# More fillers at the start, an earlier last attention product, and a smaller feed-forward share in one stage of a fused attention and feed-forward kernel

## The chip, the cores and the metric

The kernel runs on one core of a Trainium2 chip. The metric is the device time of one execution in microseconds (us). Times are medians of several runs. A ratio is the mean time of one kernel's fast runs over the mean time of the other's fast runs of the same rounds, so it is not quite the ratio of the medians that are quoted beside it.

## The reference

Grouped-query attention, then a feed-forward layer with squared ReLU, over 8 batches. There are 16 query heads and 4 key/value heads of dimension 64, and 384 positions in each batch.

```python
scores = (q @ k.T) / sqrt(64)              # k and v repeated for groups of 4 heads
attn   = softmax(scores)
x      = (attn @ v)                        # laid out as 3072 tokens x 1024
h      = maximum(x @ w_in, 0)              # w_in: 1024 x 2048
out    = (h * h) @ w_out                   # w_out: 2048 x 1024
```

The inputs and the output are 32-bit floats; the loads on the GpSimd queue convert them to bf16 on their way (the load of one batch's k, 98304 numbers, moves 192.0 KB into `k_st`), apart from the first batch's q, k and v, which are converted by engines.

## The kernel before

A helper records every operation with what it reads and writes. It puts each engine's operations in program order and adds the semaphore waits. So **each engine works strictly in the order of the program text**. Two heads make a "pair": 8 pairs per batch, numbered `n` from 0 over all batches. "b0" is batch 0 (pairs 0 to 7), "b1" batch 1 (pairs 8 to 15), "b2" batch 2.

The feed-forward of one batch lags one batch behind its attention. It is a generator of small steps: up tiles (`x @ w_in`, 8 matmuls each) and down tiles (`h² @ w_out`, 16 matmuls each). `fill(ns)` takes steps from it until their estimated time is used up. Its results alternate between two banks of PSUM (the memory that matmuls write), `f_ps0` and `f_ps1`. `xT` is the transposed attention output that the up tiles read.

```python
    PER_PAIR = {1: 3700.0, **{b: 5100.0 for b in range(2, B + 1)}}
    ...
    # b0: no feed-forward exists yet; idle(n) issues n matmuls on a zeroed tile ("fillers")
    def idle(count):
        def mm(pe):
            for _ in range(count):
                m = pe.matmul(f_ps[1][:, 0:256], warm[:, 0:128], warm[:, 0:256])
            return m
        R.add("tensor", mm, reads=["warm"], writes=[("f_ps", 1)])
    ...
    # from b1 on
    for n in range(NPB, NP + 1):                 # NPB = 8 pairs per batch
        per = PER_PAIR[n // NPB]
        if n < NP:
            scores_pair(n)                       # q k^T, then one exponential on ScalarE
        fill(per * 0.4)
        if n > NPB:
            attend(n - 1, 0)                     # attention x v on TensorE (AV)
        fill(per * 0.2)
        if n > NPB:
            attend(n - 1, 1)                     # AV, then 1/sum and product on VectorE
            landed = put_x(n - 1)                # transpose by DMA into xT, on the sync queue
            ...
        if n % NPB == 4 and n // NPB + 1 < B:
            prepare(n // NPB + 1)                # k duplicate on VectorE, then DMA transposes
        if n % NPB == 7 and n // NPB + 1 < B:
            prepare_v(n // NPB + 1)
        fill(per * 0.4)
        ready[0] = max(0, n // NPB - 1)          # whose feed-forward may start
```

A down tile ends with a copy of its bank to SBUF (the working memory on the chip) on VectorE ("y copy") and a store. The big loads all wait in one queue, in this order:

```python
    ... # w_in in 8 parts, v of b1 among them
    for i in range(2):
        load_w_out(i)
    load_k(2)
    load_q(2)
    load_v(2)
```

The softmax here doesn't subtract the row's maximum and nothing guards it: scores larger than these inputs give would overflow.

Of the kernel before, what the change touches and what calls it, by code (L numbers as in the profile page):

```python
# [106 lines left out]
def bass_gqa_attention__then__ffn_squared_relu_kernel(  # L107
# [11 lines left out]
    B, H, S, D = 8, 16, 384, 64  # L119
# [4 lines left out]
    NPB = H // 2  # L124
# [145 lines left out]
# [7 lines that stand above are left out]
# [11 lines left out]
    RING, FREE = (4, 5, 6), (0, 1, 2, 3)  # L288
# [9 lines left out]
    def turn_on_pe(src, src_keys, dst, dst_keys, banks, eng="vector", n=NJ):  # L298
        ps, key = turn_bank(banks)

        def tr(pe):
            for t in range(n):
                m = pe.matmul(ps[:, t * 128:(t + 1) * 128], src[:, t * 128:(t + 1) * 128], ident[:],  # L303
                              is_transpose=True)
            return m

        R.add("tensor", tr, reads=[*src_keys, "ident"], writes=[key])
        if eng == "scalar":
            R.add(eng, lambda e: e.copy(dst, ps[:, 0:n * 128]), reads=[key], writes=dst_keys)
        else:  # L310
            R.add(eng, lambda e: e.tensor_copy(dst, ps[:, 0:n * 128]), reads=[key], writes=dst_keys)  # L311

    def first_kT(g, b=0, banks=RING, j0=0, j1=NJ):
        turn_on_pe(k_dup[b][:, g * NJ + j0:g * NJ + j1].rearrange("p a x d -> p (a x d)"),
                   [("k_dup", b, g, j) for j in range(j0, j1)], kT[b][:, g, j0 * 128:j1 * 128],
                   [("kT", b, g, j) for j in range(j0, j1)], banks, n=j1 - j0)

    def first_qT(c, b=0, banks=RING):
        turn_on_pe(q_st[b][:, 2 * c:2 * c + 2, :].rearrange("p h e -> p (h e)"), [("q_st", b, c)],
                   qT[b][:, c], [("qT", b, c)], banks)  # L320

    def first_oT(c, banks=RING, eng="vector"):
        turn_on_pe(o_sb[c % NO].ap().rearrange("p i s d -> p (i s d)"), [("o_sb", c % NO, x) for x in range(2)],
                   xT[0][:, c], [("xT", 0, c)], banks, eng)

    def dup_all_k(b, eng="vector"):
        src = k_st[b % NKS].ap().rearrange("p g j d -> p (g j) d").unsqueeze(2)
        R.add(eng, lambda e: e.tensor_copy(  # L328
            k_dup[b % 2][:, :, :, :], src.to_broadcast([128, HKV * NJ, 2, D])),
            reads=[("k_st", b % NKS)], writes=[("k_dup", b % 2, g, j) for g in range(HKV) for j in range(NJ)])  # L330
# [26 lines left out]
    def scores_unit(p, j):  # L357
        u = (p * NJ + j) % 2
        kt, qt, keys, k_keys = operands(p)
        keys = keys + k_keys[j:j + 1]  # L360

        def sc(pe):
            for x in range(2):
                rows = slice(64 * x, 64 * x + 64)
                m = pe.matmul(sc_ps[:, 2 * u + x, 0:S], kt[rows, j * 128:(j + 1) * 128], qt[rows, :])  # L365
            return m

        R.add("tensor", sc, reads=keys, writes=[("sc", 2 * u), ("sc", 2 * u + 1)])
        src = sc_ps[:, 2 * u:2 * u + 2, 0:S].rearrange("p x (t c) -> p x t c", t=NJ)
        dst = expT[p % NEX][:, j, :].rearrange("p (t x c) -> p x t c", x=2, t=NJ)  # L370
        R.add("scalar", lambda e: e.activation(dst, src, AF.Exp, scale=0.125),  # L371
              reads=[("sc", 2 * u), ("sc", 2 * u + 1)], writes=[("expT", p % NEX, j)])
# [29 lines left out]
    def attend(p, s, alone=False):  # L402
        b, g = p // NPB, (p % NPB) // 2
        acc, acc_key = (po_alt, ("sc", 1)) if alone and s == 1 else (po_v, "po")

        def av(pe):
            for i in range(NJ):
                f = NJ * s + i
                for j in range(NJ):
                    m = pe.matmul(acc[:, i, s, :], expT[p % NEX][:, j, f * 128:(f + 1) * 128],  # L410
                                  v_aug[b % 2][:, g * NJ + j, :], start=(j == 0), stop=(j == NJ - 1))
            return m

        R.add("tensor", av, reads=[("expT", p % NEX, j) for j in range(NJ)] +
              [("v_aug", b % 2), ("v_one", b % 2)], writes=[acc_key])
        if alone or s == 1:
            ss = slice(s, s + 1) if alone else slice(0, 2)
            w = ss.stop - ss.start
            rinv_v = rinv[p % 2][:, :, ss].unsqueeze(3)
            R.add("vector", lambda e: e.reciprocal(rinv_v, acc[:, :, ss, D:D + 1]),  # L420
                  reads=[acc_key], writes=[("rinv", p % 2)])
            rb = rinv_v.to_broadcast([128, NJ, w, D])
            R.add("vector", lambda e: e.tensor_tensor(o_sb[p % NO][:, :, ss, :], acc[:, :, ss, 0:D], rb, ALU.mult),  # L423
                  reads=[acc_key, ("rinv", p % 2)], writes=[("o_sb", p % NO, s)])
# [70 lines left out]
    def all_feed_forward():  # L495
        for b in range(B):
            while ready[0] < b:
                yield None
            yield from feed_forward(b)

    ffn = all_feed_forward()
    credit = [0.0]
    PER_PAIR = {1: 3700.0, **{b: 5100.0 for b in range(2, B + 1)}}

    def fill(ns):
        credit[0] += ns
# [7 lines left out]
    turns = [lambda banks=RING, g=g: first_kT(g, 1, banks) for g in range(HKV)]  # L514
    turns += [lambda banks=RING, c=c: first_qT(c, 1, banks) for c in range(NPB)]

    idle(13)
    first_kT(0, banks=(4,), j1=1)
    idle(1)
    first_qT(0, banks=(6,))  # L520
    for n in range(NPB):
        ring = (4, 6) if n < 4 else RING
        scores_unit(n, 0)
        if n >= 4:
            turns.pop(0)()
        elif n == 0:
            first_kT(0, banks=(4,), j0=1)
            idle(2)
        else:
            idle(1)  # L530
        if n >= 1:
            attend(n - 1, 0)
        scores_unit(n, 1)
        if n % 2 == 1 and n + 1 < NPB:
            first_kT((n + 1) // 2, banks=ring)
        if n + 1 < NPB:
            first_qT(n + 1, banks=ring)
        if n == 3:
            dup_all_k(1)
        if n >= 1:  # L540
            attend(n - 1, 1)
        scores_unit(n, 2)
        if n < 4:
            idle(1)
        if n >= 2:
            first_oT(n - 2, ring)
        if n in (4, 6, 7):
            turns.pop(0)()
    for _ in range(3):
        next(ffn)  # L550
    attend(NPB - 1, 0, True)
    first_oT(NPB - 2, (4,), "scalar")
    attend(NPB - 1, 1, True)
    for _ in range(5):
        next(ffn)
    first_oT(NPB - 1, (0,))
    for _ in range(4):
        next(ffn)
    prepare_v(1)
    while turns:  # L560
# [2 lines left out]
    for n in range(NPB, NP + 1):  # L563
        per = PER_PAIR[n // NPB]
        if n < NP:
# [49 lines left out]
```

## Time and profile before

| | before |
|---|---|
| median of the first three runs | 440.08 us |
| span of the profiled run | 437.8 us |
| TensorE busy | 431.2 us |
| TensorE's waits that the profile names | 4.1 us |

PE is TensorE, PEld its weight loads, DVE VectorE, ACT ScalarE, POOL GpSimd, SPq the sync engine's DMA queue. The granted clock (PEclk) is the share of TensorE's full clock that the profile records as allowed. First the busy table and the chain of work that ended last, of the kernel before:

```profile
PE 431.2 (98%) x3631; PEld 240.7 (55%) x3631; DVE 164.3 (38%) x357; ACT 199.5 (46%) x210; POOL 34.4 (8%) x50
...
PE 97%; DVE 2%; DMA 1%; issue 0%
```

TensorE looks like the whole story. Its list of waits (waiting line, what released it, total us, times, longest us):

```profile
PE f_ps L441 <- DMA xT<-o_sb: 1.3, 1, 1.3
PE f_ps L273 <- DVE warm L221: 1.1, 1, 1.1
PE f_ps L441 <- DVE qT L311: 0.7, 1, 0.7
```

The first is the last transpose of b1's attention output, which the up tiles of b1 need. The third is a copy that must leave the bank of the first up tile. The change aims at both.

Less visible is the state of the other engines at 60 to 68 us. The timeline, before (start us, duration us, engine, line, operation, count, and in brackets idle time just before it and what ended it):

```profile
60.58 0.69 DVE L467 COPY y_sb<-f_ps 128x512 f32<-128x512 f32 x1 [3.84 <-PE f_ps L459]
...
61.41 0.56 DVE L423 TENSOR_TENSOR o_sb<-po,rinv 128x384 bf16<-128x384 f32 x1
...
65.38 1.89 PE L459 MATMUL f_ps<-w_out_sb,h2T 128*128 128x512 bf16 x8
...
65.94 0.56 DVE L328 COPY k_dup<-k_st 128x1536 bf16<-128x1536 bf16 x1 [3.98 <-DMA k_st<-in_k_dram]
66.42 0.68 DVE L467 COPY y_sb<-f_ps 128x512 f32<-128x512 f32 x1
...
67.20 0.66 PE L382 MATMUL sc_ps<-qT,kT 64*128 64x128 bf16 x9
...
67.80 1.90 PE L459 MATMUL f_ps<-w_out_sb,h2T 128*128 128x512 bf16 x8
```

VectorE stands for 3.98 us at the k duplicate, because b2's k comes late, behind all weights. This costs nothing here: the first y copy is ahead of the duplicate in program order, at 60.58 us, so its bank is free when the third down tile starts at 65.38 us. The scores at 67.20 us are those of pair 14, and the second half of that tile follows them at 67.80 us.

The loads go on up to 76 us: the DMA share is 1.23 to 1.57 in the stretches of 5 us from 41 to 76 us, and 0.99 from 76 to 81. The table by stretch, before (busy us and instructions of each engine, granted clock, DMA share, GB/s):

```profile
core 0: us, PE busy (x) PEld busy (x) DVE busy (x) ACT busy (x) POOL busy (x), PEclk, DMA share, GB/s
61.00:66.00 5.00, 5.00 (x46) 2.51 (x44) 0.99 (x4) 2.09 (x1) 0.00 (x0) 1.00 1.41 215
66.00:71.00 5.00, 5.00 (x46) 2.55 (x45) 2.99 (x7) 2.09 (x1) 0.00 (x0) 1.00 1.57 161
...
86.00:91.00 5.00, 5.00 (x46) 3.06 (x44) 2.33 (x5) 1.57 (x3) 0.00 (x0) 1.00 0.09 35
```

A share above 1 means that the times of the packets overlap: 1.57 while the loads run, 0.09 after them.

### The profile page before, as it was taken

How to read it: one execution, taken by the hardware profiler on the slowest of the kernel's cores; microseconds unless marked ns; L12 is line 12 of the kernel's file. 1: busy time of each engine (PE TensorE's matmuls, PEld its weight loads, DVE VectorE, ACT ScalarE, POOL GpSimd, SP SyncE). 2: the span in 40 equal slices, each digit the busy share in tenths (PEclk: the TensorE clock that was granted, in tenths of full speed). 3: DMA queues.
4: the chain of work that ended last, by engine and by line, in shares of the span. 5: the costliest groups of instructions: out<-in, count | busy, mean ns of one | idle time of the engine just before them, and what ended most of it. 6: DMA issues, size and time to landing. Idle time of an engine off the chain costs nothing.

```text
span 437.8 us, 8262 instructions
## 1 busy us (share of the span) xinstructions
PE 431.2 (98%) x3631; PEld 240.7 (55%) x3631; DVE 164.3 (38%) x357; ACT 199.5 (46%) x210; POOL 34.4 (8%) x50
## 2 busy tenths in 40 slices
PE   8999999899999999999999999999999999999997
PEld 4555654466545654466555565456654565545544
DVE  2555424244224442334432453234422444224412
ACT  4856753456433663256433555326642466203400
POOL 4940000020000200020000200002000000000000
PEclk9999999999999999999999999999999999999999
DMA  7999999757722937229622576229442100220012
GB/s 219 172 197 202 192 204 168 178 59 79 150 91 67 114 69 130 67 69 115 123 83 70 74 98 143 66 91 113 64 112 91 58 20 18 67 82 24 1 54 89
DMA packets 96083, 44.70 MB, mean 102 GB/s; under 512 B 74416, under 2 KB 90032, under 8 KB 96048
## 3 DMA queue, kind: packets, MB, share of 16 engines
q0 software_dynamic: 34288, 16.65, 30.5%
q1 hardware_dynamic: 58720, 25.28, 25.3%
q10 hardware_dynamic: 3040, 2.26, 1.7%
q8 instruction: 28, 0.46, 0.4%
q14 instruction: 7, 0.06, 0.0%
HBM read 35.65 MB, written 12.58 MB: 110 GB/s over the span
## 4 chain that ended last, share of the span: by engine, by line
PE 97%; DVE 2%; DMA 1%; issue 0%
PE f_ps L459 39%; PE f_ps L441 38%; PE po L410 8%; PE sc_ps L382 7%; PE sc_ps L365 1%; PE f_ps L273 1%; PE sc_ps L303 1%; PE f_ps L303 1%; DMA xT<-o_sb 1%; DVE o_sb L423 1%; DVE qT L311 0%; DVE xT L311 0%; PE sc_ps L441 0%; DVE kT L311 0%; DVE rinv L420 0%
## 5 line engine op out<-in xcount | busy, mean ns | idle before, releaser
L441 PE MATMUL f_ps<-xT,w_in_sb 128*128 128x384 bf16 x1016 | 181.4, 326 | 2.1 <-DMA xT<-o_sb 1.3
L459 PE MATMUL f_ps<-w_out_sb,h2T 128*128 128x512 bf16 (+2 forms) x784 | 180.3, 375 | 0.0
L399 ACT ACTIVATE expT<-sc_ps 128x2304 bf16<-128x2304 f32 x56 | 116.8, 2085 | 100.9 <-PE sc_ps L382 99.1
L441 PEld LDWEIGHTS f_ps<-xT,w_in_sb 128*128 128x128 bf16 x1016 | 92.4, 98 | 63.3 <-issue 6.4
L450 ACT ACTIVATE h2T<-hr 128x384 bf16<-128x384 f32 x128 | 66.6, 521 | 105.5 <-DVE hr L448 104.0
L459 PEld LDWEIGHTS f_ps<-w_out_sb,h2T 128*128 128x128 bf16 x784 | 70.2, 98 | 75.7 <-issue 5.5
L448 DVE TENSOR_SCALAR hr<-f_ps 128x384 f32<-128x384 f32 x127 | 70.5, 556 | 101.1 <-PE f_ps L441 101.1
L467 DVE COPY y_sb<-f_ps 128x512 f32<-128x512 f32 (+2 forms) x49 | 33.3, 680 | 104.9 <-PE f_ps L459 104.5
L410 PEld LDWEIGHTS po<-v_aug,expT 128*128 128x128 bf16 x1143 | 52.7, 99 | 21.7 <-ACT expT L371 0.7
L410 PE MATMUL po<-v_aug,expT 128*128 128x65 bf16 x1143 | 57.3, 195 | 0.4 <-DVE o_sb L423 0.3
L382 PE MATMUL sc_ps<-qT,kT 64*128 64x128 bf16 (+2 forms) x504 | 37.2, 272 | 0.1
L423 DVE TENSOR_TENSOR o_sb<-po,rinv 128x384 bf16<-128x384 f32 x64 | 35.5, 554 | 2.2
L382 PEld LDWEIGHTS sc_ps<-qT,kT 64*128 64x128 bf16 x504 | 20.6, 94 | 21.7 <-issue 16.1
L420 DVE RECIPROCAL rinv<-po 128x6 f32<-128x6 f32 x64 | 12.2, 191 | 44.6 <-PE po L410 44.5
L167 POOL DMA_DIRECT2D k_st<-in_k_dram x7 | 5.4, 775 | 257.5 <-DMA xT<-o_sb 257.5
L371 ACT ACTIVATE expT<-sc_ps 128x768 bf16<-128x768 f32 x24 | 18.8, 809 | 4.1 <-PE sc_ps L365 3.6
L365 PE MATMUL sc_ps<-qT,kT 64*128 64x384 bf16 x48 | 9.4, 388 | 0.5 <-DVE qT L311 0.5
L181 POOL DMA_DIRECT2D q_st<-in_q_dram x7 | 8.2, 1176 | 0.0
L273 PE MATMUL f_ps<-warm 128*128 128x256 bf16 x23 | 6.3, 397 | 1.3 <-DVE warm L221 1.1
L189 POOL DMA_DIRECT2D w_in_sb<-in_moe_w_in_dram x8 | 7.0, 888 | 0.0
L174 POOL DMA_DIRECT2D v_st<-in_v_dram x7 | 5.5, 783 | 0.0
L328 DVE COPY k_dup<-k_st 128x1536 bf16<-128x1536 bf16 x7 | 3.9, 553 | 4.0 <-DMA k_st<-in_k_dram 4.0
(44 smaller groups left out, 54.1 us busy)
## 6 DMA issues: line engine op xcount, KB each, us to landing
out_dram<-y_sb SPq DMA_DIRECT2D x47, 256.0 KB, 2.0
q_st<-in_q_dram POOLq DMA_DIRECT2D x7, 768.0 KB, 9.8
w_in_sb<-in_moe_w_in_dram POOLq DMA_DIRECT2D x8, 512.0 KB, 14.7
w_out_sb<-in_moe_w_out_dram POOLq DMA_DIRECT2D x2, 2048.0 KB, 36.2
k_st<-in_k_dram POOLq DMA_DIRECT2D x7, 192.0 KB, 3.6
v_st<-in_v_dram POOLq DMA_DIRECT2D x7, 192.0 KB, 10.4
xT<-o_sb SPq DMA_TRANSPOSE x56, 2.4
q_f<-in_q_dram ACTq DMA_DIRECT2D x1, 768.0 KB, 8.0
```

The lines of the kernel that those rows point to most:

```text
L365: m = pe.matmul(sc_ps[:, 2 * u + x, 0:S], kt[rows, j * 128:(j + 1) * 128], qt[rows, :])
L371: R.add("scalar", lambda e: e.activation(dst, src, AF.Exp, scale=0.125), reads=[("sc", 2 * u), ("sc", 2 * u + 1)], writes=[("expT", p % NE ...
L382: return pe.matmul(sc_flat[:, at + c0:at + c1], kt[rows, j * 128:(j + 1) * 128], qt[rows, c0:c1])
L399: R.add("scalar", lambda e: e.activation(dst, src, AF.Exp, scale=0.125), reads=sc_keys, writes=[("expT", p % NEX, j) for j in range(NJ)])
L410: m = pe.matmul(acc[:, i, s, :], expT[p % NEX][:, j, f * 128:(f + 1) * 128], v_aug[b % 2][:, g * NJ + j, :], start=(j == 0), stop=(j == NJ ...
L420: R.add("vector", lambda e: e.reciprocal(rinv_v, acc[:, :, ss, D:D + 1]), reads=[acc_key], writes=[("rinv", p % 2)])
L423: R.add("vector", lambda e: e.tensor_tensor(o_sb[p % NO][:, :, ss, :], acc[:, :, ss, 0:D], rb, ALU.mult), reads=[acc_key, ("rinv", p % 2)] ...
L441: m = pe.matmul(acc[:, 0:S], w_in_sb[:, kc, c * 128:(c + 1) * 128], xT[b % NXT][:, kc, :], start=(kc == 0), stop=(kc == NKC - 1))
L448: R.add("vector", lambda e: e.tensor_scalar_max(hr[r][:, :], acc[:, 0:S], 0.0), reads=[key], writes=[("hr", r)])
L450: R.add("scalar", lambda e: e.activation(h2T[b % 2][:, c, :], hr[r][:, :], AF.Square), reads=[("hr", r)], writes=[("h2T", b % 2, c)])
L459: m = pe.matmul(f_ps[u][:, 0:c1 - c0], h2T[b % 2][:, c, i * 128:(i + 1) * 128], w_out_sb[:, c, jj * 512 + c0:jj * 512 + c1], start=(c == 0 ...
L467: R.add("vector", lambda e: e.tensor_copy(y_sb[yb][:, c0:c1], f_ps[u][:, 0:c1 - c0]), reads=[("f_ps", u)], writes=[("y", yb, c0)])
```

## The change

Its three parts: six more fillers in the first pairs, meant to have TensorE's clock rise earlier (at 13.54 us in the trace of before; that fillers move it was the author's estimate, and stays open below); at the end of b0, AV of the last pair ahead of most of the opened up tiles, with transposes on other banks, so that TensorE need not wait for the copies; and 3400 instead of 3700 for the feed-forward per pair in b1, so that enough of it is left to cover the wait for the last xT.

```diff
-    PER_PAIR = {1: 3700.0, **{b: 5100.0 for b in range(2, B + 1)}}
+    PER_PAIR = {1: 3400.0, **{b: 5100.0 for b in range(2, B + 1)}}
...
-    idle(13)
+    idle(11)
     first_kT(0, banks=(4,), j1=1)
-    idle(1)
+    idle(3)
     first_qT(0, banks=(6,))
+    idle(2)
     for n in range(NPB):
-        ring = (4, 6) if n < 4 else RING
+        ring = (4, 6) if n < 4 else RING if n < 6 else (4, 5)
         scores_unit(n, 0)
         if n >= 4:
-            turns.pop(0)()
+            turns.pop(0)(ring)
         elif n == 0:
             first_kT(0, banks=(4,), j0=1)
-            idle(2)
+            idle(3)
         else:
-            idle(1)
+            idle(2 if n == 1 else 1)
...
         if n < 4:
-            idle(1)
+            idle(2 if n < 2 else 1)
...
-        if n in (4, 6, 7):
-            turns.pop(0)()
+        if n in (4, 6):
+            turns.pop(0)(ring)
+    next(ffn)
+    next(ffn)
+    attend(NPB - 1, 0, True)
+    attend(NPB - 1, 1, True)
+    first_oT(NPB - 2, (4,), "scalar")
     for _ in range(3):
         next(ffn)
-    attend(NPB - 1, 0, True)
-    first_oT(NPB - 2, (4,), "scalar")
-    attend(NPB - 1, 1, True)
-    for _ in range(5):
-        next(ffn)
     first_oT(NPB - 1, (0,))
-    for _ in range(4):
+    for _ in range(7):
         next(ffn)
```

## The prediction

> **What bounds it now.** TensorE: busy 431.2 of 437.8 us (busy table), 97% of the chain that ended last. Recorded waits of TensorE total only 4.1 us (list of waits): 1.3 us at 84.5 us (batch 1's up tiles wait for the last xT transpose), 0.7 at 27.7 us (first up tile waits for a qT copy to free its bank). In the first 28 us ScalarE paces: 24 exponentials of 0.81 us run from 5.71 to 28.15 us. TensorE is slow until 13.5 us: a pair of score matmuls takes 0.50 us in the timeline before it, 0.34 after; a filler 0.39, then 0.28.[...]
>
> A second limit is hidden until 76 us: the loads. The DMA share is 1.2 to 1.5 from 13 to 76 us. The load of batch 2's k lands at 65.8 us; VectorE, in order, sat idle 4.0 us for it (k duplicate, 65.94 us). q lands at 72.1 us, its transpose just before batch 2's first scores (76.64 us), and the sync queue is full from 72 to 85 us.
>
> **What the change does.**
> 1. Fillers: 23 to 29, a start-to-start of 0.21 us each at half clock.[...] ScalarE's three gaps of 0.44, 0.88 and 0.44 us at 9.4 to 13.6 us shrink: about 1.2 us gained.
> 2. Reordered end of b0: removes the 0.7 us wait and a 0.3 us gap before 32.5 us: about 0.9 us.
> So batch 1's first scores move from 37.9 to about 36.7 us (one more turn slot ahead of them costs 0.8).
> 3. 3400 instead of 3700 per pair: by batch 2's first scores 8 fewer down matmuls (8 x 0.2155 = 1.7 us) are done. They fill the 1.3 us wait for xT.
>
> **Why little of it reaches the end.** The loads don't move. And in the changed order VectorE's copy of the first y tile comes after the k duplicate instead of before it. The third down tile reuses that bank, so it can start only after 65.9 + 0.56 (duplicate) + 0.69 (copy) = 67.2 us; TensorE would be there at about 64.2. So 2 to 3 us of new waiting swallow steps 1 and 2. Before, the same place is at 67.80 us: 0.6 us ahead[...]. After it there is 1.7 us more work, and 1.3 us less waiting; batch 2's first scores may wait up to 0.5 us for qT, the last xT may still cost a few tenths. Sum: -0.6 to -1.2, +1.7, -1.3, +0 to +0.5: about -0.5 us.
>
> **Prediction.** 439.6 us, 8 in 10 between 438.2 and 440.9. Faster by over 2%: 0.01; within 2%: 0.98; slower: 0.01.
>
> **What would show it.** Timeline: score pairs at 0.34 us from 7 to 10 us on; last b0 exponential ending near 27 us (28.15 before). List of waits: L441 on the qT copy gone; L441 on the xT transpose gone or under 0.6 us; a new wait of L459 on VectorE's y copy (or k duplicate) of 2 to 3 us near 64 to 67 us.
>
> **What would make it wrong.** Loads landing 2 us earlier: then steps 1 and 2 survive, 437. The new wait[...] so that the clock halves again: 441 to 442.

Here and in two expectations below (experiments 2 and 7), passages are cut where the marks stand, because no trace or run of this case shows what they say. The sum came to about -0.5 us, from 440.08 to 439.6. The 1.2 us of step 1 stand as the author's estimate (steps 1 and 2 are not in the sum). "At half clock" in step 1 is what the traces show: fillers start 0.21 us apart there, and 0.11 us apart at a recorded clock of 1.00 (28 of them take 3.22 us in experiment 4).

## The result, and the profile after

| | before | changed |
|---|---|---|
| median (6 runs each) | 439.76 us | 443.15 us |
| lowest to highest | 439.23 to 440.68 | 441.00 to 444.01 |
| ratio, 95% interval | | 1.0071, 1.0047 to 1.0095 |
| span of the profiled run | 437.8 us | 441.1 us |
| mean granted clock of the profiled run | 1.00 | 0.992 |

The changed kernel is 0.7% slower, where 0.1% faster was predicted. Both waits that the change aimed at are gone (no line of the whole list has L441), and there is a new one. The list of waits of the changed kernel begins:

```profile
PE f_ps L459 <- DVE y_sb L467: 3.4, 1, 3.4
PE f_ps L273 <- DVE warm L221: 1.1, 1, 1.1
PE f_ps L273 <- DVE qT L311: 0.6, 2, 0.5
PE f_ps L303 <- POOL q_st L230: 0.6, 1, 0.6
```

The timeline of the changed kernel shows its cause (same columns as above):

```profile
58.31 1.02 PE L459 MATMUL f_ps<-w_out_sb,h2T 128*128 128x512 bf16 x4
...
58.74 0.56 DVE L423 TENSOR_TENSOR o_sb<-po,rinv 128x384 bf16<-128x384 f32 x1
...
63.98 0.66 PE L382 MATMUL sc_ps<-qT,kT 64*128 64x128 bf16 x9
...
66.84 0.56 DVE L328 COPY k_dup<-k_st 128x1536 bf16<-128x1536 bf16 x1 [7.54 <-DMA k_st<-in_k_dram]
67.31 0.68 DVE L467 COPY y_sb<-f_ps 128x512 f32<-128x512 f32 x1
...
68.05 3.17 PE L459 MATMUL f_ps<-w_out_sb,h2T 128*128 128x512 bf16 x7 [3.41 <-DVE y_sb L467]
```

The first down tile is complete on TensorE at 59.3 us. Its y copy comes at 67.31, because it now stands behind the k duplicate, for which VectorE waits 7.54 us. The third down tile needs that bank, so TensorE stands from 64.64 to 68.05 us. The trace then shows what the wait did to the clock; the table by stretch, changed kernel:

```profile
63.57:66.99 3.42, 1.07 (x12) 0.37 (x9) 0.15 (x1) 2.09 (x1) 0.00 (x0) 1.00 1.54 153
66.99:70.40 3.41, 2.35 (x6) 0.89 (x7) 2.26 (x5) 0.00 (x0) 0.00 (x0) 0.50 1.64 197
70.40:73.81 3.41, 3.19 (x18) 1.57 (x18) 0.00 (x0) 0.00 (x0) 0.00 (x0) 0.50 1.27 195
```

From 66.99 to 73.81 us the granted clock is 0.50. In the timeline the seven recorded down matmuls at 68.05 (the record of one of eight is missing) take 3.17 us, where eight took 1.90 us before. The half clock lasts 6.82 us, two stretches of 3.41 us. The same step fits the rest of this trace's clock record: the clock rose at 5.55 us, 61.44 us before the fall, which is 18 times 3.413 us. The stretch before the fall was not idle throughout: 1.07 of its 3.42 us were busy.

The accounts of the two profiled runs meet. At the down matmuls that follow pair 14's scores the changed kernel is 0.25 us later (68.05 against 67.80). There it starts its third down tile, of which the kernel before has done half. From there to the end it needs 373.05 us against 370.0. The 3.05 us more are roughly: 8 down matmuls not yet done (8 x 0.2155 = 1.7 us), less the xT wait saved (1.3 us), plus half of the 5.76 us from there to the end of the half clock (2.9 us). The last is an estimate from the lines above, which takes TensorE as working all that time, at half its speed (four down matmuls take 1.90 us at 71.95 us, at clock 0.50, and 1.02 us at 74.01 us, at 1.00). The sum, 3.3 us, is 0.25 over what was measured.

The clock also separates the runs: five of the six have a mean clock of 0.992 and take 442.86 to 444.01 us; the one with 0.996 took 441.0 us. In the profiled run 0.992 is 6.82 us at half (0.5 x 6.82 / 441.1 = 0.008); by the same sum 0.996 is about 3.41 us at half. Two cautions belong to this column. A trace without a clock record also reads 1.0: those of experiments 8 and 9 have none, though in experiment 8 score pairs went from 0.50 to 0.34 us. And the kernel before is not free of it: 7 of its 32 runs beside the experiments read 0.996, where in the run is not known, because none of them kept a trace.

### The profile page after: what moved, and what is told of

Same layout as the page of the kernel before. It is cut to its first block, busy times and chain, and to the rows that moved or that the text cites. A ratio compares the mean times of both kernels' runs of the same rounds, so it can differ in the third digit from the quotient of the medians.

```text
span 441.1 us, 8239 instructions
## 1 busy us (share of the span) xinstructions
PE 429.7 (97%) x3602; PEld 240.6 (55%) x3637; DVE 164.8 (37%) x357; ACT 199.4 (45%) x210; POOL 34.2 (8%) x50
## 4 chain that ended last, share of the span: by engine, by line
PE 84%; DMA 11%; POOL 4%; issue 1%; DVE 0%; ACTq 0%
PE f_ps L459 37%; PE f_ps L441 34%; DMA k_st<-in_k_dram 10%; PE po L410 7%; PE sc_ps L382 7%; POOL w_in_sb L189 2%; DMA v_f<-in_v_dram 1%; POOL q_st L230 1%; POOL w_out_sb L195 1%; POOL k_dup L235 0%; POOL q_st L181 0%; DVE y_sb L467 0%; ACTq L207 0%; POOL v_aug L242 0%; POOL k_st L167 0%
## 5 line engine op out<-in xcount | busy, mean ns | idle before, releaser
L459 PE MATMUL f_ps<-w_out_sb,h2T 128*128 128x512 bf16 (+2 forms) x749 | 178.4, 378 | 5.4 <-DVE y_sb L467 3.4
L441 PE MATMUL f_ps<-xT,w_in_sb 128*128 128x384 bf16 x1016 | 181.8, 326 | 0.0
L441 PEld LDWEIGHTS f_ps<-xT,w_in_sb 128*128 128x128 bf16 x1016 | 92.6, 98 | 60.2 <-issue 6.1
L365 PE MATMUL sc_ps<-qT,kT 64*128 64x384 bf16 x48 | 8.1, 333 | 0.1
```

Of the source, the lines that this page charges most:

```text
L441: m = pe.matmul(acc[:, 0:S], w_in_sb[:, kc, c * 128:(c + 1) * 128], xT[b % NXT][:, kc, :], start=(kc == 0), stop=(kc == NKC - 1))
L459: m = pe.matmul(f_ps[u][:, 0:c1 - c0], h2T[b % 2][:, c, i * 128:(i + 1) * 128], w_out_sb[:, c, jj * 512 + c0:jj * 512 + c1], start=(c == 0 ...
```

## The experiments

Theory A: the smaller share in b1 turns the order of y copy and k duplicate round on VectorE; this makes the wait, and the wait halves the clock. Theory B, the rival: the fillers or the reorder at the end of b0 cost the time. Each call of runs had its own runs of the kernel before, on the same chip.

### 1. Only the share undone

```diff
-    PER_PAIR = {1: 3400.0,      # in the changed kernel
+    PER_PAIR = {1: 3700.0,
```

> The changed kernel with 3700 put back in b1 (fillers and reorder kept). Theory A (the smaller share in b1 puts the first y copy behind the k duplicate on VectorE; TensorE then waits over 3.4 us and its clock halves for 6.8 us): no wait of L459 on the y copy, no stretch at half clock near 67 to 74 us, k duplicate still at 66 to 67 us, the wait for the last xT comes back at 1.3 to 2.3 us, and the time is 439.0 to 440.3, at least 2.5 us under the changed kernel. Theory B (the fillers or the reorder at the end of b0 cost the time): stays at 442 to 444.

Measured: 439.35 us against 440.16, ratio 0.9988 (0.9969 to 1.0008), all four runs at clock 1.0. The y copy is ahead of the duplicate again; timeline of this run:

```profile
58.53 0.69 DVE L467 COPY y_sb<-f_ps 128x512 f32<-128x512 f32 x1 [3.19 <-PE f_ps L459]
...
66.77 0.56 DVE L328 COPY k_dup<-k_st 128x1536 bf16<-128x1536 bf16 x1 [6.02 <-DMA k_st<-in_k_dram]
```

The whole loss is gone with one number put back. Theory B falls: fillers and reorder are still in. The wait for the last xT is back at 1.0 us (1.3 to 2.3 were expected).

### 2. Only the share changed

```diff
-    PER_PAIR = {1: 3700.0,      # in the kernel before
+    PER_PAIR = {1: 3400.0,
```

> The kernel before with only 3700 -> 3400. Theory A: VectorE has the same changed order, so TensorE waits for the y copy, but arrives 0.9 us later than in the changed kernel: a wait of 1 to 2.5 us[...]; no wait for xT; 439.8 to 441. Theory B: no loss from this part, the xT wait of 1.3 us is gone: 438.3 to 439.

Measured: 438.86 us (438.09 to 440.63) against 440.16, ratio 0.9977 (0.9953 to 1.0002): a time under the range that theory A gave, and not clearly different from before. The order on VectorE is turned and the wait is there, 2.94 us in the profiled run, but all four runs kept clock 1.0. The line of the wait, and two stretches of that run on a grid of 3.41 us (17 and 18 such steps after the rise of its clock at 4.95 us):

```profile
68.19 1.04 PE L459 MATMUL f_ps<-w_out_sb,h2T 128*128 128x512 bf16 x4 [2.94 <-DVE y_sb L467]
```

```profile
62.97:66.38 3.41, 2.29 (x17) 0.96 (x15) 0.00 (x0) 1.08 (x1) 0.00 (x0) 1.00 1.89 139
66.38:69.79 3.41, 1.60 (x16) 0.89 (x17) 2.42 (x5) 1.02 (x1) 0.00 (x0) 1.00 1.81 186
```

So the part to blame is harmless by itself: a wait of 2.94 us fell across two stretches of the grid and left 1.60 us of work in the emptier one. In the changed kernel the earlier arrival from the other parts lengthened the wait to 3.41 us. Whether the length of the wait or its place on the grid kept the clock up in these four runs was not tested.

### 3. b2's k loaded earlier

```diff
-    for i in range(2):
-        load_w_out(i)
-    load_k(2)
+    load_w_out(0)
+    load_k(2)
+    load_w_out(1)
     load_q(2)
```

> The changed kernel with the load of batch 2's k put ahead of the second half of w_out in the same queue. Theory A: k lands near 52 to 54 us, VectorE no longer waits for it, the wait for the y copy is gone, the clock stays up; batch 2's first scores then wait for qT up to about 2 us (its q load lands as late as ever); 437.8 to 439.5. Theory B: 442 to 444, whatever becomes of the wait.

Measured: 442.25 us, ratio 1.0052 (1.0037 to 1.0067), all four runs at 0.996. This missed the expected range, and by the time alone it looks like theory B; the profile says otherwise. The wait for the y copy is gone, the duplicate starts at 59.41 us without any idle time. But TensorE ran on into the next late load. Its list of waits begins:

```profile
PE sc_ps L382 <- issue: 3.2, 1, 3.2
```

These are b2's first scores, for which TensorE stands from 73.68 to 76.88 us. The profile names no releaser, but they read qT, whose DMA transposes are late. The stretches of this run:

```profile
74.59:78.00 3.41, 1.12 (x12) 0.65 (x13) 0.41 (x1) 0.41 (x1) 0.00 (x0) 1.00 1.14 215
78.00:81.41 3.41, 3.41 (x10) 1.23 (x9) 0.00 (x0) 1.69 (x1) 0.00 (x0) 0.50 0.90 181
```

Half clock again, for 3.41 us. The loads still go on to 74 us, when b2's v lands. The transposes of q were issued from 73.03 us on, against 70.90 in the changed kernel. That moving k forward delayed them is not shown: in the other runs they were issued between 70.54 and 73.90 us.

### 4. The wait filled with fillers

28 fillers on a free bank just before the scores of pair 14, in the place of the wait (its core):

```diff
+        if n == 14:
+            idle_on_sc(28)
         if n < NP:
             scores_pair(n)
```

> The changed kernel with 28 more filler matmuls (3.0 us of TensorE, on a bank that is free) ahead of the scores of pair 14, just before the wait; they take the place of the wait and add nothing to the work that must be done. Theory A, clock part: the y copy still comes at 67.3 us and the first down matmul after it at about 68.0, but no stretch at half clock follows; 439.4 to 440.4. If the wait itself and not the clock is what costs: no better than 442.5.

Measured: 441.1 us, ratio to before 1.0019 (1.0004 to 1.0034), all four runs at clock 1.0: the halved clock is gone, though the third down tile starts even later than in the changed kernel:

```profile
64.64 3.22 PE L281 MATMUL sc_ps<-warm 128*128 128x256 bf16 x28
67.79 0.66 PE L382 MATMUL sc_ps<-qT,kT 64*128 64x128 bf16 x9
68.67 1.67 PE L459 MATMUL f_ps<-w_out_sb,h2T 128*128 128x512 bf16 x7 [0.22 <-DVE rinv L420]
```

The gain over the changed kernel, 2.05 us by the medians (2.3 us by the ratios, each against its own runs of before; 2.4 us by the spans of the profiled runs), is 0.7 us short of the expected range. The estimate of 2.9 us for the clock, less the 0.6 us by which the third down tile starts later here (68.67 against 68.05), gives 2.3 us. So the halved clock was most of the 3.4 us that the change lost.

### 5. The k duplicate one pair later

```diff
-        if n % NPB == 4 and n // NPB + 1 < B:
+        if n % NPB == (5 if n < 2 * NPB else 4) and n // NPB + 1 < B:
             prepare(n // NPB + 1)
```

> The changed kernel with batch 2's k duplicate and transposes one pair later in program order (after the first y copy and pair 12's normalisation). Theory A: TensorE no longer waits for the first y copy and runs on, full clock, to batch 2's first scores at about 73.2 us, where it waits some 2 us for qT (its load lands as late as ever); no half clock; 437.8 to 439.4. If the load order alone sets the end (as with k first), the wait for qT is over 3 us and the clock halves there: 441 to 442.5.

Measured: 440.34 us against 440.03, ratio 1.0005 (0.9968 to 1.0042): over the range expected. The wait for the y copy is gone, and as expected TensorE waits 2.3 us for qT. In the profiled run the clock was then half for 3.41 us, which was not expected; one other run also reads 0.996, without a trace to say where, and the remaining two 1.0.

```profile
PE sc_ps L382 <- DMA qT<-q_st: 2.3, 1, 2.3
```

```profile
73.17:76.58 3.41, 1.33 (x13) 0.75 (x14) 0.56 (x1) 0.62 (x1) 0.00 (x0) 1.00 1.07 213
76.58:79.99 3.41, 3.41 (x10) 1.24 (x9) 0.00 (x0) 1.47 (x1) 0.00 (x0) 0.50 0.52 155
```

### 6. And pair 15's products ahead of b2's first scores

The edit of experiment 5, and for pair 16 only:

```diff
-        if n < NP:
+        if n < NP and n != 2 * NPB:
             scores_pair(n)
         fill(per * 0.4)
...                                  # attend(n - 1, ...), put_x(n - 1)
+        if n == 2 * NPB:
+            scores_pair(n)
         fill(per * 0.4)
```

> The kernel of e5 with, for pair 16 only, the attention matmuls and fill of pair 15 ahead of the scores of pair 16. Theory A (TensorE is bound, the late loads only matter where it stands idle for them): the wait for qT goes too, no wait of over 0.6 us between 30 and 90 us; 436.2 to 438.0. If the loads bound the end in any order, a wait of 2 us or more comes back at the first scores of batch 2 or at the last xT, and it stays at 438 to 440.

Measured: 438.1 us against 440.03, ratio 0.9947 (0.9919 to 0.9976), clock 1.0 in all runs. The longest wait between 30 and 90 us is 0.4 us:

```profile
PE f_ps L273 <- DVE warm L221: 1.1, 1, 1.1
PE f_ps L273 <- DVE qT L311: 0.5, 1, 0.5
PE po L410 <- DVE o_sb L423: 0.4, 1, 0.4
PE sc_ps L382 <- ACT expT L399: 0.4, 1, 0.4
```

With both late arrivals given work to cover them, the kernel beats both of the others. The median is 0.1 us over the expected range. The ratio flatters it: three of the seven runs of before on this chip read clock 0.996. Against the other four (mean 439.74 us) it is 0.996, near the 0.997 of experiment 12.

### 7. The filler that waits for the copy it was to cover

In the changed kernel the two fillers ahead of the first scores write the bank that the qT copy still reads, so they start at 5.31 us, after the copy, and push the first scores from 5.17 to 5.73 us. Here they use another bank, on top of experiment 6:

```diff
-    idle(2)
+    idle_on_sc(2)
     for n in range(NPB):
```

> The kernel of e6 with the two fillers ahead of the very first scores on a bank of the scores instead of the one that the qT copy reads. They no longer wait for that copy: first scores at 5.2 instead of 5.73 us, last exponential of b0 0.3 to 0.5 us earlier; 0.2 to 0.5 us under e6[...].

Measured: 438.36 us, ratio 0.9946 (0.9916 to 0.9976). The first scores start at 5.28 us, and the last exponential ends 0.7 us earlier than in experiment 6 (27.19 against 27.88), though the clock also rose earlier in this trace (score pairs take 0.34 us from 6.49 us on, in experiment 6 from 10.04). The time is that of experiment 6. Waits of 0.7 us for xT and 0.5 us for qT have come back: the loads again.

### 8. Only the fillers

> The kernel before with the fillers of the change alone. Clock rises near 5.5 to 7 us instead of 13.5; batch 1's first scores 0.2 to 0.6 us earlier than 37.9; the order on VectorE is that of before, so no wait for the y copy; the wait for the last xT grows by what was gained; 439.3 to 440.4, the same as before. If the fillers were to blame for the loss: 442 or more.

The edit is that of the change to all `idle` lines, in the kernel before. Measured: 439.23 us against 440.03, ratio 0.9971 (0.9943 to 0.9999). Not to blame, and worth little. b1's first scores start at 37.46 us (37.88 before). Contrary to what was expected, score pairs still took 0.50 us at 8.16 us in this trace and 0.34 only from 9.19.

### 9 and 10. What the share, and the start, are worth once the waits are covered

Experiment 9 is experiment 6 with 3700:

> The kernel of e6 with 3700 instead of 3400 in b1: is the smaller share worth anything once its two waits are gone? Theory A: yes, as the change intended: with 3700 the feed-forward of b0 runs out before the last xT lands and a wait of 0.7 to 1.8 us for it comes back near 82 to 84 us; 438.6 to 439.8, that is 0.5 to 1.7 us over e6. If the share is worthless: no wait and the time of e6 (437.5 to 438.5).

Measured: 437.94 us against 439.98, ratio 0.9951 (0.993 to 0.9971), no slower than experiment 6. A wait did come back, but of another kind: 1.2 us of the scores of pair 17 for the exponential of pair 16.

Experiment 10 is experiment 6 with the kernel before's fillers and its end of b0:

> The kernel before with the two repairs of e6 and 3400, but with its own fillers and its own end of b0. Theory A: the 0.85 us that fillers and reorder gained at the start reach the end once nothing waits for the loads, so this kernel is 0.4 to 1.2 us over e6, at 438.5 to 439.3, with the first scores of b1 at 37.7 to 38.0 us as before. If the loads still set the end, it is the same as e6 within 0.3 us.

Measured: 438.46 us, ratio 0.9972 (0.9944 to 1.0), an interval that overlaps that of experiment 9, so it did not settle the matter. Its profile upset a reading of mine: b1's first scores start at 36.87 us, not 37.7 to 38.0. The clock had risen at 6.24 us here, with the very fillers with which it rose at 13.54 us in the profile of before.

### 11 and 12. The repairs with and without the change, five rounds on one chip

Experiment 11 puts the two repairs of experiment 6 into the kernel before. Experiment 12 is experiment 6 again.

> The kernel before with the two repairs of e6 only: 3700, its own fillers, its own end of b0. If the three parts of the change are worth their 0.85 us of earlier start and 1.3 us of saved waiting once the repairs are in: 438.8 to 439.8, at least 0.5 us over e12. If the repairs do it all: within 0.4 us of e12.

> The kernel of e6 once more, on the same chip as e11: 437.5 to 438.6, with an interval against the kernel before that lies wholly below 0.998.

Measured: 439.08 us and 438.91 us against 440.29; ratios 0.9972 (0.996 to 0.9984) and 0.997 (0.9959 to 0.9982). They are the same: nothing of the change's three parts can be seen on top of the repairs, within intervals of about 0.5 us to each side. How the repairs alone gain their 1.2 us is not shown. The profiled run of experiment 11 is 0.7 us shorter than that of before (437.1 against 437.8), but 0.56 us of this are there at b1's first scores (37.32 against 37.88), which no repair touches; its clock had risen at 4.50 us instead of 13.54. In experiment 6 most of the gain does come later: 0.77 us at that place (37.11), 2.5 us at the end. In these two traces k came later (duplicate at 68.93 and 67.83 us, against 65.93 in experiment 6), though experiments 9 and 10, on the same chip, had it at 66.81 and 66.25. In both profiled runs TensorE again waits 0.7 us for the last xT. Experiment 12's median is 0.3 us over the range expected, and the upper end of its interval, 0.9982, is just not under 0.998.

## Why the prediction was wrong

**Right: the mechanism and the place.** The y copy behind the k duplicate, the third down tile as the one that waits, the start of its wait ("about 64.2", measured 64.64) and both removed waits came out as written. Experiments 1 and 5 show that the order on VectorE makes the wait, experiment 4 that the wait brings the half clock. VectorE kept to the program's order in this trace: a y copy ready at 59.3 us ran at 67.31. That the loads do not come earlier was right too: the duplicate began at 66.84 us (65.94 before), with a DMA share of 1.54 and 1.64 in the two stretches around it.

**Wrong: two terms of the sum.** The failing step is "So 2 to 3 us of new waiting swallow steps 1 and 2", with the third tile at 67.2 us.

- The wait was 3.41 us, and ended at 68.05 instead of 67.2. The k duplicate started 0.9 us later than in the trace of before. This start is not fixed: over the profiled runs in which it waited for the k load, it lay between 65.93 and 68.93 us. I took one trace's figure as the load's arrival, and even reckoned with an earlier one.
- The clock term, zero in my sum, was about 2.9 us by the estimate from the trace (experiment 4: 2.05 us by the medians, while its third tile started 0.6 us later). I named this risk ("so that the clock halves again: 441 to 442"), but left it out of the range, and the length of wait that I gave for it did not hold. Waits of 2.3 us (experiment 5) and 3.2 us (experiment 3) were followed by half clock too, while 2.94 us (experiment 2) was not. A wait of 2 to 3 us should have been priced with the clock loss.

Together the two terms are 0.85 + 2.9 = 3.75 us, against a miss of 3.55 us (443.15 against 439.6).

**Wrong too, but not what made it slower: the gain at the start.** Predicted were 1.2 us from the clock and 0.9 us from the reorder, with b1's first scores at 36.7 us. Measured was 37.03 against 37.88 in the first two traces. The fillers before the first scores wait for the copy they were to cover; the first scores came 0.56 us later for it. And the rise of the clock is not the fillers' doing alone: with the old ones it came at 13.54, 4.95, 6.24 and 4.50 us in four traces (the first score pair of 0.34 us started at 14.05, 5.22, 6.38 and 5.15 us); with the new ones that pair started between 5.57 us (experiment 5) and 10.56 us (experiment 4) in eight traces. Whether the new fillers move it on average stays open: four traces with the old ones are too few.

**Where the intended gains went.** The two removed waits are real, but TensorE's lead is of use only while its next work has arrived. In the changed kernel it ran into the load of k; when that was repaired, into the load of q (experiment 5); then partly into the last xT (experiments 7 and 12). The smaller share sharpened this: it leaves 8 down matmuls, 1.7 us of work that depends on none of these loads, undone while TensorE stands waiting for one of them.

## What to carry to other kernels

Before moving work between stages of in-order engines, read what each engine does next to its longest wait for a load: an operation that slips behind that wait takes its bank with it. When TensorE is to arrive earlier somewhere, ask which arrival it then meets, and put work there that depends on nothing still to come; the kernels whose intervals lie clearly below 1 here all do so (experiments 6, 7, 9, 11 and 12), though the trace of experiment 11 does not show where its gain arose. Price a TensorE wait of 2.3 us or more (the shortest that was followed by half clock here; 3.2 and 3.41 us were too, 2.94 us was not) with the clock that it may halve, and take the arrival of a load as a range over several traces.

## What the traces show of the clock

- Stretches of 3.41 us with 1.07 (changed kernel), 1.12 (experiment 3) and 1.33 us (experiment 5) of TensorE busy time were followed by half clock, and one with 1.60 us (experiment 2) was not. Whether the profile's busy time is what decides, and where in between a limit would lie, is open.
- In the profiled run of experiment 5 half clock followed a gap of 2.3 us. After the 3.41 us gap of the changed kernel the clock stayed at half for 6.82 us; TensorE was busy for 2.35 us of the first 3.41 us and 3.19 us of the second.
- With the same fillers the clock rose at 4.50, 4.95, 6.24 and 13.54 us in four traces. In the last of them TensorE was busy for 3.39 of 3.41 us from 6.71 to 10.12 us, yet score pairs at 11.79 and 13.05 us still took 0.50 us.
- The granted clock in the profile reads 1.00 before its first recorded event, and throughout where no event is recorded. In the trace of before, a pair of score matmuls takes 0.50 us before the first event at 13.54 us and 0.34 us afterwards. The trace of experiment 8 has no event, though its score pairs went from 0.50 us at 8.16 us to 0.34 us at 9.19 us.
